# First MoE with two products a stage instead of three, and w2 times w_out folded into one matrix on the chip

## The chip, the cores and the metric

The kernel runs on one core of a Trainium2 chip. The metric is the device time of one execution in microseconds. A core has TensorE (matrix products), the vector engine (DVE), ScalarE (ACT), GpSimd (POOL) and SyncE (SP), each with a queue of its own that it works off in order; they wait for each other by semaphores.

## The reference

Three layers follow each other. The first is a linear attention with a decaying complex state, over 4 batches, 8 heads, 768 steps and head size 48. Its output, 3072 tokens of 384 numbers, goes into the first MoE, which the change is about, and the result into the second MoE, where each token goes to one of 8 experts.

```python
def _moe_ref(x, w1, w2, w3, w_out):
    h = np.maximum(np.maximum(x @ w1, x @ w2), x @ w3)
    return (h @ w_out).astype(np.float32)
```

Here x is 3072 x 384, w1, w2 and w3 are 384 x 768, w_out is 768 x 384. The weights come in as 64-bit floats. All is computed in 32 bits.

## The kernel before, in words

The program has two phases. In `phase1` the 3072 tokens are worked off as 12 units of 256 tokens (`NU`, `W`): attention, then the first MoE. In `phase2` the second MoE runs in blocks of tokens of one expert. The change touches `phase1` alone.

A unit passes `front` (the scale of the decay), `mid` and `back` (running products of the decay, the vector engine's share, which end in the tile `QK`), DMAs that lay `QK` out by head as `S`, and `attn`, twice, for 128 tokens each. In `attn` TensorE turns keys (`pk`, copied to `kt`), forms scores (`pa`, masked by the vector engine into `at`), the state (`pT`) and the output (`py`). The output leaves as two parts: `xhi`, rounded to the format fp32r, and the rest `xlo`. Products in fp32r are used in threes (high x high, high x low, low x high), so that three of them do for one in full fp32.

`moe1` computes a unit's first MoE in three stages `f2` of 256 hidden units. For each of the three weights `m` and each half `f` of the stage, `mm` issues 9 products (3 pairs of parts x 3 blocks of 128 inputs) of 128 x 128 weights by 256 tokens into a PSUM tile `ph`. ScalarE copies the first `ph` to `h`, the vector engine takes two maxima. In stages 0 and 1 (`SPLIT` is 2) `h` is rounded to `hhi`, the vector engine subtracts it (`hlo`), and 3 products per block with w_out's parts `wohi`, `wolo` add to `px`; in stage 2 the product with `wo` is in plain fp32. `px` has 392 columns: 384 outputs and 8 (`pG`) that give the second MoE's logits. ScalarE takes it out to `x1s`, and a DMA writes it to memory, from where the second MoE gathers its tokens.

```python
for n, (w, x, i) in enumerate((w, x, i) for w, x in ((self.whi, xhi), (self.wlo, xhi), (self.whi, xlo))
                              for i in range(3)):
    t.matmul(o, w[m, i][:, c], x[:, i], start=n == 0, stop=n == 8)
```

`weights` runs at the start. It loads 24 blocks of 128 x 384 64-bit numbers (6 of w_out, 18 of the three weights), puts each together as 32-bit floats on ScalarE and the vector engine (`sg`, `f`, `h`: sign, exponent, fraction), and splits 22 of them: ScalarE rounds (`hi`), TensorE forms the block minus `hi` in PSUM (`pd`), ScalarE takes that out (`rest`). It also turns w_out (`pwt`, `wt`) for the 8 extra columns.

Nothing is issued in the order of the code. A `Recorder` keeps all calls of `phase1`, a planner sorts them per engine by a list of keys, and `BIAS` shifts the keys of kinds of operations (a name of a tile and an engine's letter). Where the plan has TensorE idle for long, `keep_warm` (line 627) puts in products of the identity. Every instruction that the planner issues has line 368 in the profile.

Of the kernel before, what the change touches and what calls it, by code (L numbers as in the profile page):

```python
# [9 lines left out]
F32 = mybir.dt.float32  # L10
F32R = mybir.dt.float32r
# [3 lines left out]
AF = mybir.ActivationFunctionType  # L15
# [6 lines left out]
W = 256  # L22
# [3 lines left out]
DM = H * D  # L26
# [5 lines left out]
L = 8  # L32
# [91 lines left out]
class Recorder:  # L124
# [203 lines left out]
    def issue(self):  # L328
# [30 lines left out]
        for i in seq:  # L359
# [9 lines left out]
        return max(end)  # L369

    ENGINES = "vector", "scalar", "tensor", "gpsimd", "sync"
    BIAS = {"Gs": 1.84, "QKrg": -1.81, "Sg": 1.17, "Ss": 0.07, "Tss": 0.78, "Xv": 0.43, "arenv": 0.65, "cvhv": 0.53,
            "embss": -0.15, "fms": 2.46, "fmv": 3.34, "fyv": 0.76, "h_s": 0.7, "h_v": -0.65, "kt_s": -0.33, "pa_t": 1.07,
            "ph__t": -0.59, "pk_t": 1.3, "px__t": 0.15, "rrs": -0.38, "rrv": -0.75, "rwhig": -0.62, "rwlog": 1.88,
            "sav": -0.63, "slott": 2.08, "whi_s": 0.47, "wlo_s": 1.99, "xhis": 1.21, "xss": 0.26}
    PASSES, WAIT, LANES = 4, 130.0, 8
    START = {"vector": 1600.0, "gpsimd": 2200.0, "scalar": 2500.0, "sync": 1000.0}
    WINDOW = 4096 / 1.2
# [4 lines left out]
class Prog:  # L383
# [325 lines left out]
    def weights(self, split=True):  # L709
# [17 lines left out]
        spots = [(m, i) for i in range(3) for m in range(3)]  # L727
        todo = [(self.io["wo"][i], None, i, None) for i in range(6)]
        todo += [(self.io["w123"][m, i, :, c:c + n], m, i, c) for m, i in spots for c in (0, n)]
        sq = self.tl(pm, [128, 2 * W], "h", 2, "embsq")[:E, :DM]  # L730
        nrm, sr = [self.tl(pm, [E, 1], nm, 1, nm) for nm in ("nrm", "nrms")]
        s.activation(sq, emb, AF.Square, accum_out=nrm)
# [9 lines left out]
        ring, first = 0, 2 * self.SPLIT if split else 0  # L742
        for k, (src, m, i, c) in enumerate(todo):

            spot = None
            if split and m is not None:
# [24 lines left out]
            whole = m is None and i >= first  # L771
            o = self.wo[:, i - first, :DM] if whole else f if split else self.w[:, m, i, c:c + n]
            v.scalar_tensor_tensor(o.bitcast(I32), raw[:, :, 0], 29, h, op0=ALU.logical_shift_right, op1=ALU.bitwise_or)
            if split and not whole:
                if m is not None and c == 0:
# [3 lines left out]
                hi, rest = (self.wohi[:, i, :DM], self.wolo[:, i, :DM]) if m is None else \  # L779
                    (self.whi[m, i][:, c:c + n], self.wlo[m, i][:, c:c + n])  # L780
                s.copy(hi, f)
                pd = self.tl(self.pf, [128, n], "h", 3, f"pd{k}")
                with q.group():
                    t.matmul(pd, self.ident, f, start=True, stop=False)
                    t.matmul(pd, self.minus, hi, start=False, stop=True)
                s.copy(rest, pd)
            if m is None:

                if i == 0:
                    pG = self.tl(self.pf, [128, 6, E], "x1", 2, "pG")  # L790
                pt = self.tl(self.pf, [128, 3, 128], "h", 3, f"pwt{k}")
                for j in range(3):
                    t.transpose(pt[:, j], o[:, j * 128:(j + 1) * 128], self.ident)
                wt = self.tl(pm, [128, 3, 128], "h", 2, f"wt{k}")
                s.copy(wt, pt)
                for j in range(3):
                    t.matmul(pG[:, i], wt[:, j], enT[:, j], start=j == 0, stop=j == 2)
            if m is None and i == 5:
                if first:
                    s.copy(self.wohi[:, :, DM:], pG[:, :first])  # L800
                    v.tensor_sub(self.wolo[:, :, DM:], pG[:, :first], self.wohi[:, :, DM:].bitcast(F32))
                if first < 6:
                    v.tensor_copy(self.wo[:, :, DM:], pG[:, first:])

    def sqrt_small(self, new, out, x, n):

# [11 lines left out]
    def moe1(self, u):  # L818
# [5 lines left out]
        def mm(o, m, f):  # L824
            c = slice(f * 128, (f + 1) * 128)
            with q.group():
                for n, (w, x, i) in enumerate((w, x, i) for w, x in ((self.whi, xhi), (self.wlo, xhi), (self.whi, xlo))
                                              for i in range(3)):
                    t.matmul(o, w[m, i][:, c], x[:, i], start=n == 0, stop=n == 8)
        px = [self.tl(self.pf, [128, XC], "x1", 2, f"px1_{u}_{i}") for i in range(2)]  # L830
        for f2 in range(3):
            ps = []
            for m in range(3):
                ps.append(self.tl(self.pf, [128, 2, W], "h", 3, f"ph{u}_{f2}_{m}"))
                for f in range(2):
                    mm(ps[m][:, f], m, 2 * f2 + f)
            h = self.tl(pm, [128, 2, W], "h", 2, f"h{u}_{f2}")
            key, q.key = q.key, u + self.KEYS["max"]
            s.copy(h, ps[0])
            v.tensor_max(h, ps[1], h)  # L840
            v.tensor_max(h, ps[2], h)
            if f2 >= self.SPLIT:
                q.key = key
                for tt in range(2):
                    with q.group():
                        for f in range(2):
                            t.matmul(px[tt], h[:, f, tt * 128:tt * 128 + 128], self.wo[:, 2 * (f2 - self.SPLIT) + f],
                                     start=f2 + f == 0, stop=f2 + f == 3)
                continue
            hi = self.tl(pm, [128, 2, W], "hhi", 1, f"hhi{u}_{f2}", F32R)  # L850
            s.copy(hi, h)
            lo = self.tl(pm, [128, 2, W], "h", 2, f"hlo{u}_{f2}", F32R)
            v.tensor_sub(lo, h, hi.bitcast(F32))
            q.key = key
            for tt in range(2):
                with q.group():
                    for f in range(2):
                        ts = slice(tt * 128, tt * 128 + 128)
                        wh, wl = self.wohi[:, 2 * f2 + f], self.wolo[:, 2 * f2 + f]
                        for k, (a, b) in enumerate(((hi, wh), (hi, wl), (lo, wh))):  # L860
                            t.matmul(px[tt], a[:, f, ts], b, start=f2 + f + k == 0, stop=f2 + f + k == 5)
# [188 lines left out]
    def phase1(self):  # L1050
        nc, tc = self.nc, self.tc
        with ExitStack() as ctx:
# [9 lines left out]
            self.wo = mw.tile([128, 6 - 2 * self.SPLIT, XC], F32, name="wo")  # L1062
            self.wohi = mw.tile([128, 2 * self.SPLIT, XC], F32R, name="wohi")
            self.wolo = mw.tile([128, 2 * self.SPLIT, XC], F32R, name="wolo")
# [660 lines left out]
def host_layout(i):  # L1725
    f = np.ascontiguousarray

    def tr(x):
# [10 lines left out]
    perm = [h * D + e for h, e in XROWS]  # L1739

    w123 = np.stack([i[f"moe_w{n}"][perm].reshape(3, 128, FF) for n in (1, 2, 3)]).view(np.int64)
    wo = i["moe_w_out"].reshape(6, 128, DM).view(np.int64)
    return {
        "a": f(a), "qk": f(qk), "v": f(v), "w123": f(w123), "wo": f(wo),
        "emb": f(i["moe2_expert_emb"]),
        "tau": f(i["moe2_tau"]).reshape(1, 1),
        "w21": f(i["moe2_w1"].reshape(E, DM // 128, 128, FF2).transpose(0, 2, 1, 3)).reshape(E, 128, -1),
# [14 lines left out]
```

## Time and profile before

| | us |
|---|---|
| median of 3 runs | 809.39 (806.94 to 810.66) |
| the profiled execution | 811.25 |
| its span, first to last instruction | 809.4 |
| busy: TensorE / vector engine / ScalarE / GpSimd | 750.9 / 630.2 / 445.2 / 100.5 |
| mean granted TensorE clock | 0.977 |

The span is what the trace covers; 1.85 us of the execution lie outside. "Busy" is the time in which at least one instruction of the engine ran. The trace's products overlap each other (one of 392 columns lasts 0.34 us, and the next starts sooner): what one costs is the distance from one start to the next. PEld is TensorE's loading of weights, PEclk its granted clock (1.00 is 2.4 GHz).

### The profile page before, as it was taken

The page shows a single profiled execution, that of the slowest core. Times are in us where ns is not written, and L with a number is a line of the kernel's source. Part 1 is how long each engine was busy: PE and PEld are TensorE (multiplying, and loading weights), DVE is VectorE, ACT ScalarE, POOL GpSimd, SP SyncE. Part 2 cuts the span into 40 slices and gives each one's busy share as a digit, 9 for nine tenths or more (in the row PEclk, how much of TensorE's full clock was granted, in tenths as well). Part 3 has the DMA queues.
Part 4 walks back from the last instruction along what each step waited for, and adds up shares of the span by engine and source line. Part 5 has one row for each costly group of instructions (what it writes and reads, how often), then busy time and mean ns, then how long its engine had stood idle before and what let it go on. Part 6 is the DMA issues. An engine that isn't in the chain of part 4 may idle for free. (4 is left out here: it accounts for less than half of the span.)

```text
span 809.4 us, 19242 instructions
## 1 busy us (share of the span) xinstructions
PE 750.9 (93%) x7705; PEld 690.7 (85%) x7705; DVE 630.2 (78%) x1244; ACT 445.2 (55%) x1018; POOL 100.5 (12%) x156
## 2 busy tenths in 40 slices
PE   1757899999999999999999999999999999999996
PEld 0635789989898989999898989889989898989885
DVE  8999999999999999999988822659996455555420
ACT  8998746646647465665355341228545456554521
POOL 6301000000000000000000000021113312223111
PEclk9778999999999999999999999999999999999998
DMA  9706262571717345261624060051029694782500
GB/s 360 286 1 157 38 157 65 137 184 32 186 52 150 93 108 135 66 143 59 151 70 102 14 110 2 21 216 41 28 81 420 217 387 145 255 341 74 179 21 25
DMA packets 28754, 107.46 MB, mean 133 GB/s; under 512 B 5060, under 2 KB 8179, under 8 KB 25568
## 3 DMA queue, kind: packets, MB, share of 16 engines
q1 hardware_dynamic: 20432, 77.55, 32.2%
q0 software_dynamic: 7952, 28.21, 10.6%
q8 instruction: 62, 1.02, 0.5%
q10 hardware_dynamic: 272, 0.39, 0.2%
q14 instruction: 36, 0.29, 0.1%
HBM read 96.35 MB, written 10.62 MB: 132 GB/s over the span
## 5 line engine op out<-in xcount | busy, mean ns | idle before, releaser
L368 PE MATMUL ph<-xhi,whi 128*128 128x256 f32 x648 | 118.4, 291 | 0.4 <-DVE h L368 0.4
L368 PE MATMUL ph<-xlo,whi 128*128 128x256 f32 x648 | 113.0, 283 | 0.6 <-DVE xlo L368 0.6
L368 PE MATMUL ph<-xhi,wlo 128*128 128x256 f32 x648 | 112.7, 283 | 0.0
L368 PEld LDWEIGHTS ph<-xhi,whi 128*128 128x128 f32 x648 | 93.3, 191 | 6.9 <-issue 3.5
L368 PEld LDWEIGHTS ph<-xlo,whi 128*128 128x128 f32 x648 | 93.1, 192 | 1.0 <-DVE xlo L368 1.0
L368 PEld LDWEIGHTS ph<-xhi,wlo 128*128 128x128 f32 x648 | 93.0, 191 | 0.0
L1312 PE MATMUL ph<-xh,w1s 128*128 128x256 f32 x264 | 77.7, 294 | 0.0
L1274 DVE TENSOR_TENSOR w2l<-queue_q_buf,w2h 128x768 fp32r<-128x768 f32 x52 | 47.9, 955 | 37.3 <-ACT w2h L1273 37.3
L1312 PE MATMUL ph<-xh,w1l 128*128 128x256 f32 x264 | 75.4, 286 | 0.0
L1312 PE MATMUL ph<-xl,w1s 128*128 128x256 f32 x264 | 75.3, 285 | 0.0
L1328 PE MATMUL py<-w2h,hlo 128*128 128x384 f32 x200 | 67.1, 336 | 3.0 <-DVE hlo L1317 3.0
L1328 PE MATMUL py<-w2h,hhi 128*128 128x384 f32 x200 | 68.5, 343 | 0.0
L1328 PE MATMUL py<-w2l,hhi 128*128 128x384 f32 x200 | 67.1, 335 | 0.0
L368 DVE TENSOR_TENSOR h<-ph,h 128x512 f32<-128x512 f32 x72 | 49.5, 688 | 16.4 <-PE ph L368 15.0
L368 POOL DMA_DIRECT2D v<-v x24 | 13.0, 540 | 391.5 <-PE py L368 389.6
L1317 DVE SCALAR_TENSOR_TENSOR hlo<-ph,hhi 128x512 fp32r<-128x512 f32 x50 | 34.3, 687 | 32.7 <-ACT hhi L1316 32.6
L1316 ACT ACTIVATE hhi<-ph 128x512 fp32r<-128x512 f32 x50 | 29.9, 598 | 48.5 <-PE ph L1312 48.3
L1312 PEld LDWEIGHTS ph<-xh,w1s 128*128 128x128 f32 x264 | 51.2, 194 | 3.8 <-issue 3.1
L1312 PEld LDWEIGHTS ph<-xh,w1l 128*128 128x128 f32 x264 | 51.2, 194 | 0.5
L1312 PEld LDWEIGHTS ph<-xl,w1s 128*128 128x128 f32 x264 | 51.2, 194 | 0.0
L368 PE MATMUL pa<-S 112*128 112x128 f32 x384 | 49.1, 277 | 1.3 <-DVE at L368 0.7
L1273 ACT CAST w2h<-queue_q_buf 128x768 fp32r x52 | 40.7, 832 | 16.6 <-PE py L1328 15.5
(401 smaller groups left out, 1818.2 us busy)
## 6 DMA issues: line engine op xcount, KB each, us to landing
queue_q_buf<-w SPq DMA_DIRECT2D x26, 1536.0 KB
S<-QK SPq DMA_DIRECT2D x46, 289.1 KB
X<-a SPq DMA_DIRECT2D x11, 768.0 KB
QKr<-qk SPq DMA_DIRECT2D x11, 768.0 KB
w1m<-w SPq DMA_DIRECT2D x5, 1536.0 KB
w2m<-w SPq DMA_DIRECT2D x5, 1536.0 KB
v<-v POOLq DMA_DIRECT2D x24, 224.0 KB, 4.4
x1d<-x1s SPq DMA_DIRECT2D x22, 192.0 KB
```

Source lines behind the costliest of these rows:

```text
L368: getattr(getattr(self.nc, c[0]), c[1])(*c[2], **c[3])
L1273: s.copy(hi, b[:, c])
L1274: v.tensor_sub(lo, bv[:, c], hi.bitcast(F32))
L1312: t.matmul(ph[:, f], a, b, start=o == 0, stop=o == len(ops) - 1)
L1316: s.activation(hi, ph, AF.Relu).ins,
L1317: v.scalar_tensor_tensor(lo, ph, 0.0, hi.bitcast(F32), op0=ALU.max, op1=ALU.subtract).ins]
L1328: t.matmul(py, a[:, f, r], c[:, k % 4], start=o == 0, stop=o == 3 * KF - 1)
```

## The change

For each element max(a, b, c) = b + max(0, a - b, c - b). So h w_out = x (w2 w_out) + max(0, x (w1 - w2), x (w3 - w2)) w_out. The kernel now forms V = w2 w_out (384 x 392, with the 8 extra columns) on the chip, as parts `vhi` and `vlo`, and keeps w1 - w2 and w3 - w2 in place of the weights. The host hands in w2 turned (`w2t`), still as 64-bit floats. In `weights` the six blocks of w2 are converted first, the twelve of w1 and w3 then, and the six of w_out last. A difference is formed in PSUM: the identity times the block, plus three turned products of w2's blocks by -1. `rest` rounds it from PSUM (`hi`), adds -hi with one product, and takes the rest out. w_out is kept whole, and four of its six blocks also in two parts, formed by ScalarE and the vector engine. V takes 18 products in plain fp32.

In `moe1` there are two `ph` a stage. ScalarE's copy of the first becomes a relu; the vector engine takes one maximum. `by_v` adds x V to `px`, 18 products a unit: first in the unit, for unit 0 last (`late`). `BIAS` is another table, so the order is made anew.

```diff
@@ weights @@
-        todo = [(self.io["wo"][i], None, i, None) for i in range(6)]
+        out = [(self.io["wo"][i], None, i, None) for i in range(6)]
+        if split:
+            spots = [(m, i) for i in range(3) for m in (0, 2)]
+            todo = [(self.io["w2t"][f], 1, f, None) for f in range(6)]
...
+        todo = todo + out
...
+        def rest(hi, lo, ps):
+            s.copy(hi, ps)
+            t.matmul(ps, self.minus, hi, start=False, stop=True, skip_group_check=True)
+            s.copy(lo, ps)
...
-                s.copy(hi, f)
                 pd = self.tl(self.pf, [128, n], "h", 3, f"pd{k}")
                 with q.group():
-                    t.matmul(pd, self.ident, f, start=True, stop=False)
-                    t.matmul(pd, self.minus, hi, start=False, stop=True)
-                s.copy(rest, pd)
+                    t.matmul(pd, self.ident, f, start=True, stop=True)
+                    for b in range(3):
+                        t.matmul(pd[:, b * 128:(b + 1) * 128], w2t[:, c // 128 + b, i * 128:(i + 1) * 128],
+                                 self.minus.bitcast(F32), start=False, stop=True, skip_group_check=True)
+                rest(self.whi[m, i][:, c:c + n], self.wlo[m, i][:, c:c + n], pd)
...
+        for f in range(2 * self.SPLIT):
+            s.copy(self.wohi[:, f], self.wo[:, f])
+            v.tensor_sub(self.wolo[:, f], self.wo[:, f], self.wohi[:, f].bitcast(F32))
+        for i in range(3):
+            pw = self.tl(self.pf, [128, XC], "h", 3, f"pw{i}")
+            with q.group():
+                for f in range(6):
+                    t.matmul(pw, w2t[:, f, i * 128:(i + 1) * 128], self.wo[:, f], start=f == 0, stop=f == 5)
+            rest(self.vhi[:, i], self.vlo[:, i], pw)
@@ moe1 @@
+        late = u == 0
+        def by_v():
+            for tt in range(2):
+                ts = slice(tt * 128, tt * 128 + 128)
+                with q.group():
+                    for n, (x, w, i) in enumerate((x, w, i) for x, w in ((xhi, self.vhi), (xhi, self.vlo), (xlo, self.vhi))
+                                                  for i in range(3)):
+                        t.matmul(px[tt], x[:, i, ts], w[:, i], start=n == 0 and not late, stop=n == 8 and late)
+        if not late:
+            by_v()
         for f2 in range(3):
             ps = []
-            for m in range(3):
+            for m in (0, 2):
...
-            s.copy(h, ps[0])
+            s.activation(h, ps[0], AF.Relu)
             v.tensor_max(h, ps[1], h)
-            v.tensor_max(h, ps[2], h)
...
+        if late:
+            by_v()
```

**What moves.** First TensorE, at the start of unit 0's attention. `pd` are splits of weights, `pwt` and `pG` belong to w_out's 8 extra columns, `pw` are V's products, `pk` and `pa` unit 0's turned keys and scores. Before:

```order
L368 MATMUL pk_1_265<-ident,S_142 128x112 x4
L368 MATMUL pa_1_269<-S_142 128x128 x4
L368 MATMUL pd_221<-cvh_154,ident 128x384
L368 MATMUL pd_221<-whi_219,minus 128x384
L368 MATMUL pk_0_263<-ident,S_142 128x112 x4
L368 MATMUL pd_223<-cvh_155,ident 128x384
L368 MATMUL pd_223<-whi_219,minus 128x384
L368 MATMUL pa_0_267<-S_142 128x128 x4
```

Of the change:

```order
L368 MATMUL pwt_214<-ident,wo 128x128 x3
L368 MATMUL pG<-enT,wt_213 128x8 x2
L368 MATMUL pG<-enT,wt_215 128x8 x3
L368 MATMUL pw_216<-wo,w2t 128x392 x6
L368 MATMUL pw_217<-wo,w2t 128x392 x6
L368 MATMUL pk_0_247<-ident,S_144 128x112 x4
L368 MATMUL pw_218<-wo,w2t 128x392 x6
L368 MATMUL pa_0_251<-S_144 128x128 x4
L368 MATMUL pk_1_249<-ident,S_144 128x112 x4
```

Unit 0's attention ran between the splits of the last weights; now all splits, w_out and two thirds of V stand ahead of it.

Then the vector engine, from the last `QK` of unit 11 on. `hlo`, `h` are unit 9's and unit 10's first MoE, `at` masked scores, `xlo` the low part of unit 10's input. Before:

```order
L368 TENSOR_TENSOR QK_1029<-rr_1028,X_891 128x6x128 x2
L368 TENSOR_TENSOR hlo_1_931<-h_1_929,hhi_1_930 128x512
L368 TENSOR_TENSOR at_0_982<-pa_0_981,mask 128x512
L368 TENSOR_TENSOR at_1_984<-pa_1_983,mask 128x512
L368 TENSOR_TENSOR h_2_935<-ph_2_1_933,h_2_935 128x512
L368 TENSOR_TENSOR h_2_935<-ph_2_2_934,h_2_935 128x512
L368 SCALAR_TENSOR_TENSOR xlo_975<-py_985,xhi_974 128x3x128
L368 TENSOR_TENSOR h_0_994<-ph_0_1_992,h_0_994 128x512
L368 TENSOR_TENSOR h_0_994<-ph_0_2_993,h_0_994 128x512
```

Of the change:

```order
L368 TENSOR_TENSOR QK_980<-rr_979,X_848 128x6x128 x2
L368 TENSOR_TENSOR hlo_1_886<-h_1_884,hhi_1_885 128x512
L368 TENSOR_TENSOR at_0_936<-pa_0_935,mask 128x512
L368 TENSOR_TENSOR at_1_938<-pa_1_937,mask 128x512
L368 TENSOR_TENSOR h_2_889<-ph_2_2_888,h_2_889 128x512
L368 SCALAR_TENSOR_TENSOR xlo_929<-py_939,xhi_928 128x3x128
L368 TENSOR_TENSOR at_0_989<-pa_0_988,mask 128x512
L368 TENSOR_TENSOR at_1_991<-pa_1_990,mask 128x512
L368 TENSOR_TENSOR h_0_947<-ph_0_2_946,h_0_947 128x512
```

The same work stands at the same place behind unit 11's `QK`, with one maximum a stage instead of two; unit 11's first scores have moved ahead of unit 10's maxima. In the whole queue 58 maxima stood ahead of this `QK`, and 29 do now.

## Rows read from the trace of the kernel before

**Rows 1.** By stage: us, busy PE PEld DVE ACT POOL, PEclk, DMA share, GB/s.
```profile
0.00:98.50 98.50, 60.45 (x468) 46.38 (x469) 91.70 (x221) 86.59 (x218) 24.11 (x75) 0.86 0.48 170
98.50:545.40 446.90, 439.63 (x5369) 408.41 (x5369) 385.27 (x761) 225.52 (x603) 15.87 (x25) 1.00 0.42 102
545.40:809.40 264.00, 250.83 (x1872) 235.92 (x1870) 153.26 (x264) 133.13 (x200) 60.53 (x56) 0.98 0.45 170
```

**Rows 2.** Timeline of TensorE where stages meet: start, us, engine, line, instruction, [idle before].
```profile
98.26 0.44 PE L368 MATMUL pd<-whi,minus 128*128 128x384 f32 x1 [0.44 <-ACT whi L368]
98.54 0.52 PE L368 MATMUL ph<-xhi,whi 128*128 128x256 f32 x3
...
545.38 10.88 PE L1312 MATMUL ph<-xT,w1s 128*128 128x128 f32 x96
```

**Rows 3.** Timeline of TensorE in the first MoE of units 9 and 11.
```profile
442.65 0.52 PE L368 MATMUL ph<-xhi,whi 128*128 128x256 f32 x3
443.01 0.52 PE L368 MATMUL ph<-xhi,wlo 128*128 128x256 f32 x3
...
532.83 0.34 PE L368 MATMUL px<-wohi,hhi 128*128 128x392 f32 x1
...
534.80 0.34 PE L368 MATMUL px<-wohi,hlo 128*128 128x392 f32 x1
...
540.36 2.79 PE L368 MATMUL px<-wo,h 128*128 128x392 f32 x8
542.99 0.49 PE L368 MATMUL pxg<-ident,xg 128*128 128x128 f32 x3
```

**Rows 4.** Vector engine's groups to 540 us: busy us, mean ns | idle before.
```profile
L368 DVE TENSOR_TENSOR h<-ph,h 128x512 f32<-128x512 f32 x72 | 49.5, 688 | 16.4 <-PE ph L368 15.0 <-ACT h L368 0.7
...
L368 DVE TENSOR_TENSOR hlo<-h,hhi 128x512 fp32r<-128x512 f32 x24 | 16.5, 689 | 8.2 <-ACT hhi L368 8.2
```

**Rows 5.** Timeline of the vector engine, a maximum and the instruction behind it.
```profile
414.65 0.68 DVE L368 TENSOR_TENSOR h<-ph,h 128x512 f32<-128x512 f32 x1
415.25 0.95 DVE L368 TENSOR_TENSOR QKr<-QKr,rr 128x768 f32<-128x768 f32 x1
```

**Rows 6.** Timeline of the vector engine, `QK` of units 0 and 11.
```profile
64.03 0.96 DVE L368 TENSOR_TENSOR QK<-rr,X 128x768 f32<-128x768 f32 x1
...
462.19 1.83 DVE L368 TENSOR_TENSOR QK<-rr,X 128x768 f32<-128x768 f32 x2
...
474.37 0.56 DVE L368 SCALAR_TENSOR_TENSOR xlo<-py,xhi 128x384 fp32r<-128x384 f32 x1 [4.50 <-ACT xhi L368]
```

**Rows 7.** Timeline of TensorE in the first stage.
```profile
24.80 0.78 PE L368 MATMUL pwt<-ident,S 128*128 128x128 f32 x3
25.41 0.29 PE L368 MATMUL pG<-enT,wt 128*128 128x8 f32 x2
...
71.16 0.81 PE L368 MATMUL pd<-S,ident 128*128 128x384 f32 x2
71.51 0.63 PE L368 MATMUL pd<-whi,minus 128*128 128x384 f32 x1
```

**Rows 8.** TensorE by 5 us in the first stage: busy, clock, DMA.
```profile
35.00:40.00 5.00, 4.98 (x26) 0.50 0.01 3
70.00:75.00 5.00, 2.57 (x15) 1.00 1.03 216
```

**Rows 9.** Timeline of the vector engine at the end of routing.
```profile
532.28 0.17 DVE L368 TENSOR_SCALAR srcrow<-arena 128x8 int32<-128x8 f32 x1
...
542.25 3.41 DVE L1266 COPY w1s<-queue_q_buf 128x1536 f32 x2 [2.80 <-DMA xg<-x1d,srcrow]
```

**Rows 10.** Groups of ScalarE: copy, rounding, and the second MoE's relu.
```profile
L1316 ACT ACTIVATE hhi<-ph 128x512 fp32r<-128x512 f32 x50 | 29.9, 598 | 48.5 <-PE ph L1312 48.3
L368 ACT COPY h<-ph 128x512 f32<-128x512 f32 x36 | 21.1, 585 | 35.2 <-DVE hlo L368 21.4 <-PE ph L368 12.1 <-DVE G L368 1.6
L368 ACT CAST hhi<-h 128x512 fp32r<-128x512 f32 x24 | 14.9, 619 | 41.3 <-PE px L368 23.1 <-DVE h L368 17.9
```

More of the change, by code (lines that the diff above doesn't have):

```diff
@@ L371 @@
     ENGINES = "vector", "scalar", "tensor", "gpsimd", "sync"
[L372 to L375, printed above, removed]
+    BIAS = {"QKrg": 0.03, "QKrv": -1.09, "QKs": -0.04, "Sg": 0.06, "Ss": -0.01, "Sv": -0.98, "Xg": -1.06, "arenv": -0.17,
+            "embss": 0.11, "embv": -0.35, "enTv": 0.06, "end_s": -0.27, "fms": 0.76, "fmv": -0.06, "fys": -0.13,
+            "hlo_v": -0.76, "lgs": 0.57, "nrmss": -0.19, "nrmsv": -0.1, "rrv": -0.58, "rwlog": 0.04, "sqrev": -0.19,
+            "takev": -0.17, "whi_s": -0.52, "wlo_s": 0.39, "wohis": -0.43, "wov": -0.9, "wts": -0.37, "xhis": -0.42}
     PASSES, WAIT, LANES = 4, 130.0, 8
@@ L726, in weights @@
         hs = [part(4 + i) for i in range(3)] + [self.tl(pm, [128, XC], "x1s", 2, f"cvh{i}")[:, :n] for i in range(2)]
-        spots = [(m, i) for i in range(3) for m in range(3)]
-        todo = [(self.io["wo"][i], None, i, None) for i in range(6)]
+        out = [(self.io["wo"][i], None, i, None) for i in range(6)]
+        if split:
+            spots = [(m, i) for i in range(3) for m in (0, 2)]
+            todo = [(self.io["w2t"][f], 1, f, None) for f in range(6)]
+            w2t = self.tl(self.pp, [128, 3, L, 3 * NR], "X", 3, "w2t").rearrange("p c l b -> p (c l b)")
+            w2t = w2t.rearrange("p (f d) -> p f d", f=6)
+        else:
+            spots, todo = [(m, i) for m in range(3) for i in range(3)], []
         todo += [(self.io["w123"][m, i, :, c:c + n], m, i, c) for m, i in spots for c in (0, n)]
+        todo = todo + out
         sq = self.tl(pm, [128, 2 * W], "h", 2, "embsq")[:E, :DM]
@@ L741, in weights @@
         v.tensor_copy(enT, ps)
-        ring, first = 0, 2 * self.SPLIT if split else 0
+        ring = 0
+        def rest(hi, lo, ps):
+            s.copy(hi, ps)
+            t.matmul(ps, self.minus, hi, start=False, stop=True, skip_group_check=True)
+            s.copy(lo, ps)
         for k, (src, m, i, c) in enumerate(todo):
             spot = None
-            if split and m is not None:
+            if split and c is not None:
                 j = spots.index((m, i)) + (c > 0)
@@ L770, in weights @@
             v.scalar_tensor_tensor(h, h, 3, sg, op0=ALU.logical_shift_left, op1=ALU.bitwise_or)
-            whole = m is None and i >= first
-            o = self.wo[:, i - first, :DM] if whole else f if split else self.w[:, m, i, c:c + n]
+            o = self.wo[:, i, :DM] if m is None else f if split and c is not None else w2t[:, i] if split else \
+                self.w[:, m, i, c:c + n]
             v.scalar_tensor_tensor(o.bitcast(I32), raw[:, :, 0], 29, h, op0=ALU.logical_shift_right, op1=ALU.bitwise_or)
-            if split and not whole:
-                if m is not None and c == 0:
+            if split and c is not None:
+                if c == 0:
                     j = spots.index((m, i))
@@ L778, in weights @@
                                                       for x in ("hi", "lo")]
-                hi, rest = (self.wohi[:, i, :DM], self.wolo[:, i, :DM]) if m is None else \
-                    (self.whi[m, i][:, c:c + n], self.wlo[m, i][:, c:c + n])
-                s.copy(hi, f)
                 pd = self.tl(self.pf, [128, n], "h", 3, f"pd{k}")
                 with q.group():
-                    t.matmul(pd, self.ident, f, start=True, stop=False)
-                    t.matmul(pd, self.minus, hi, start=False, stop=True)
-                s.copy(rest, pd)
+                    t.matmul(pd, self.ident, f, start=True, stop=True)
[3 more added lines that the diff above has]
+                rest(self.whi[m, i][:, c:c + n], self.wlo[m, i][:, c:c + n], pd)
             if m is None:
@@ L798, in weights @@
             if m is None and i == 5:
[L799 to L803, printed above, removed]
+                v.tensor_copy(self.wo[:, :, DM:], pG)
+        if not split:
+            return
+        for f in range(2 * self.SPLIT):
[7 more added lines that the diff above has]
+            rest(self.vhi[:, i], self.vlo[:, i], pw)
     def sqrt_small(self, new, out, x, n):
@@ L830, in moe1 @@
         px = [self.tl(self.pf, [128, XC], "x1", 2, f"px1_{u}_{i}") for i in range(2)]
+        late = u == 0
[8 more added lines that the diff above has]
+            by_v()
         for f2 in range(3):
             ps = []
-            for m in range(3):
+            for m in (0, 2):
                 ps.append(self.tl(self.pf, [128, 2, W], "h", 3, f"ph{u}_{f2}_{m}"))
                 for f in range(2):
-                    mm(ps[m][:, f], m, 2 * f2 + f)
+                    mm(ps[-1][:, f], m, 2 * f2 + f)
             h = self.tl(pm, [128, 2, W], "h", 2, f"h{u}_{f2}")
             key, q.key = q.key, u + self.KEYS["max"]
-            s.copy(h, ps[0])
+            s.activation(h, ps[0], AF.Relu)
             v.tensor_max(h, ps[1], h)
-            v.tensor_max(h, ps[2], h)
[L842 to L853, printed above, removed]
+            if f2 < self.SPLIT:
+                hi = self.tl(pm, [128, 2, W], "hhi", 1, f"hhi{u}_{f2}", F32R)
+                s.copy(hi, h)
+                lo = self.tl(pm, [128, 2, W], "h", 2, f"hlo{u}_{f2}", F32R)
+                v.tensor_sub(lo, h, hi.bitcast(F32))
             q.key = key
@@ L858, in moe1 @@
                         ts = slice(tt * 128, tt * 128 + 128)
-                        wh, wl = self.wohi[:, 2 * f2 + f], self.wolo[:, 2 * f2 + f]
-                        for k, (a, b) in enumerate(((hi, wh), (hi, wl), (lo, wh))):
-                            t.matmul(px[tt], a[:, f, ts], b, start=f2 + f + k == 0, stop=f2 + f + k == 5)
+                        if f2 < self.SPLIT:
+                            wh, wl = self.wohi[:, 2 * f2 + f], self.wolo[:, 2 * f2 + f]
+                            terms = (hi, wh), (hi, wl), (lo, wh)
+                        else:
+                            terms = (h, self.wo[:, 2 * f2 + f]),
+                        for k, (a, b) in enumerate(terms):
+                            t.matmul(px[tt], a[:, f, ts], b, start=late and f2 + f + k == 0,
+                                     stop=not late and f2 + f == 3 and k == len(terms) - 1)
+        if late:
+            by_v()
         for tt in range(2):
@@ L1061, in phase1 @@
             self.mw, self.whi, self.wlo = mw, {}, {}
-            self.wo = mw.tile([128, 6 - 2 * self.SPLIT, XC], F32, name="wo")
-            self.wohi = mw.tile([128, 2 * self.SPLIT, XC], F32R, name="wohi")
-            self.wolo = mw.tile([128, 2 * self.SPLIT, XC], F32R, name="wolo")
+            self.wo = mw.tile([128, 6, XC], F32, name="wo")
+            self.vhi, self.vlo = [mw.tile([128, 3, XC], F32R, name=n) for n in ("vhi", "vlo")]
+            if self.SPLIT:
+                self.wohi, self.wolo = [mw.tile([128, 2 * self.SPLIT, XC], F32R, name=n) for n in ("wohi", "wolo")]
             self.minus = self.tl(self.pm, [128, 128], "hhi", 1, "minus", F32R)
@@ L1741, in host_layout @@
     w123 = np.stack([i[f"moe_w{n}"][perm].reshape(3, 128, FF) for n in (1, 2, 3)]).view(np.int64)
+    w2t = f(i["moe_w2"][perm].T).reshape(6, 128, DM).view(np.int64)
     wo = i["moe_w_out"].reshape(6, 128, DM).view(np.int64)
     return {
-        "a": f(a), "qk": f(qk), "v": f(v), "w123": f(w123), "wo": f(wo),
+        "a": f(a), "qk": f(qk), "v": f(v), "w123": f(w123), "w2t": w2t, "wo": f(wo),
         "emb": f(i["moe2_expert_emb"]),
```

## The prediction, made before the change had run

> **What bounds the kernel now.** I read the busy time by stage first [rows 1], then the timeline of TensorE for where the stages meet and how fast it issues [rows 2, 3], then the groups and the timeline of the vector engine [rows 4 to 6], then the start of the program [rows 7, 8], and last the hand-over to the second MoE [rows 9].
>
> There are three stages. Up to 98.5 us the weights are converted and unit 0's attention runs: the vector engine is busy 91.7 of 98.5 us and ScalarE 86.6, TensorE only 60 [rows 1]. From 98.5, where the first `ph` product of unit 0 starts right behind the last split of a weight, to 545.4, where the first product of the second MoE starts [rows 2], TensorE is busy 439.6 of 446.9 us [rows 1]. So this stage, attention and first MoE of the units, goes at TensorE's pace; a product that is taken out of it shortens it, as long as its operands keep coming. They come from the vector engine, and that is the second thing to see: 385.3 us busy in the same stage, but nearly full until its last scan work (`QK` of unit 11) ends at 464 [rows 6], and idle for most of the 81 us after. It has next to no room either. The third stage, 264 us, is the second MoE; the change leaves its code and order alone, and I take it as it is.
>
> **TensorE, part by part.** One `ph` product takes 0.12 us: three start 0.36 us apart as a row of three [rows 3]. A unit has 3 stages of 3 weights, 2 halves and 9 products, 162 in all; without w2 it has 108. Removed: 54 x 0.12 = 6.48 us a unit. Added: x V, for 2 halves of the tokens 9 products of 392 columns each. Products of that form start 0.179 us apart (11 steps from 532.83 to 534.80 [rows 3]), so 18 x 0.179 = 3.22 us. Net -3.26 us a unit, **-39.1 us for 12 units**, all on the engine that sets the stage. The order as built bears it out: each unit has 12 groups of `ph`, not 18, and the 18 products by V.
>
> **The vector engine.** One of two maxima a stage goes: 36 in all. A maximum lasts 688 ns [rows 4], but the next instruction starts 0.60 us after it [rows 5], so 36 x 0.60 = 21.6 us. Four subtractions of 392 columns come in for w_out's low part; a subtraction of 512 lasts 689 ns [rows 4], so they cost at most 2.8. The loads, bit operations and their count (24 blocks of 384 columns) stay. What counts is what stands ahead of unit 11's `QK` in the queue: 58 maxima before, 29 now, so 17.4 us less, and 2.4 more by four subtractions at 0.60: **-15 us**. `QK` of unit 11 then ends at about 449 instead of 464, and up to 4 us sooner if the vector engine's own waits in that stretch (on products and on ScalarE) shrink with a TensorE that is less behind.
>
> **ScalarE.** Copy becomes relu on the same tile: 585 ns for the copy, 598 for a relu of 128x512 out of PSUM in the second MoE [rows 10]; 36 x 13 ns on an engine that is busy 225.5 of 446.9 us [rows 1] costs nothing. In the start, 22 blocks were split by two copies each; now 12 are, plus 4 copies for w_out and 6 for V: ten fewer. If this cover were gone it would be 10 x 0.5 us, a gain.
>
> **The start.** Here something is added in front. Each weight difference needs three turned products by -1 (36 of them); three turns start 0.61 us before the next instruction [rows 7], so 36 x 0.2 = 7.3 us. Ten pairs of split products go, each about 0.8 to 1.0 us (0.35 to the second, which lasts 0.63 [rows 7]): 8 to 10 us. These cancel. New is V: 18 products of w2's blocks with w_out in plain fp32. Such a product is two records of about 0.33 us (8 records for 4 products in the 2.63 us from 540.36 to 542.99 [rows 3]), so 18 x 0.66 = **11.8 us**. Twelve of the 18 stand ahead of unit 0's first turns (`pk`), and unit 0's products by V are put at the end of its first MoE. The conversion of w_out is now the last and its last block stands six bit operations behind `QK` of unit 0, which ended at 65 [rows 6]; so V cannot start before about 70 us. Not hidden at the least 0 (TensorE is busy only 60 of 98.5 us in this stage), at the most 11.8 at the full clock. The vector engine has some thirty instructions of unit 1 in its queue for that time, but then stands at the mask of unit 0's scores. I take **+6**, the middle, since the work ahead is on both sides.
>
> **The end of the stage.** Unit 11's first MoE is 3.26 us shorter, and the routing of the first 22 tiles runs beside it: its rows are ready at 532.3 and the weights of the second MoE at 542.25 [rows 9], so that only some 3 us lie between the weights and the first product at 545.4. Routing does not get shorter with unit 11's products. It starts a little sooner (the order sets part of unit 11's attention behind unit 10's last products), so 0 to 3 us of the gain are lost here; I take 2.
>
> **The sum.** By TensorE alone: -39.1 + 6 + 2 = -31. By the vector engine: the low half of unit 10's input (`xlo`) stands behind unit 11's `QK` in its queue, and came at 474.4, 71 us ahead of the second MoE [rows 6, 2]. In the change its `QK` ends at 445 to 449, `xlo` follows five instructions later, at about 453; from there two first MoEs are left, 71 - 6.5 = 64.5 us. That puts the second MoE at 517.5, a gain of 28. Both bounds are so near each other that the later rules: **-28 us**. The profiled execution took 811.25 us, of which 1.85 lie around its span of 809.4; it stands 1.9 above the median of 809.39. So 783 for it, and **781 us** against the median.
>
> **The rivals.**
> - *TensorE alone sets the pace.* V is wholly hidden in the start and the vector engine sheds its waits: -39.1 + 2 = -37, so 772 (768 to 776). For it: TensorE's idle time in the first stage. Against it: the vector engine has 15 to 19 us less to do ahead of unit 11, not 37.
> - *The vector engine alone sets it*, and its waits stay: -15 and nothing more, 794 (790 to 800). For it: it is full until 464. Against it: some of its idle time there was waiting for products.
> - *V runs at half the clock.* From 35 to 40 us TensorE was busy 4.98 of 5 us and had a granted clock of 0.50, the 1.2 GHz level, while 70 to 75 us shows 1.00, the 2.4 GHz level, with it busy 2.57 of 5 [rows 8]. If V falls into such a stretch it takes 23.6 us, 12 more, and unit 0's attention comes as much later: 793 (787 to 797). The Trainium skill (TensorE: Matmul & The Clock Gate, Part 1) has it the other way: the clock is throttled by default and sustained activity releases it. By that rule V, the densest work of the start, would be at the full level and this rival falls. The row from 35 to 40 us speaks against it: there a busy engine stayed at the lower level for all five us.
> - *Slower: the chain behind the maximum is laid bare.* With two products a stage instead of three, TensorE has 36 `ph` products of the next stage (4.3 us), not 54 (6.5 us), to run while the maximum (0.69), the rounding (0.62) and the subtraction (0.69) go by, 2.0 us [rows 4, 10]. If queues on ScalarE and the vector engine stretch that by as much as the cover lost, each of the 24 split stages waits up to 2.0 us: +48, 829. It decides from 28 / 24 = 1.2 us a stage. Against it: 4.3 us of cover for 2.0 us of work, V's products and the attention of the next unit are there as well, and a third PSUM buffer is now free for running ahead.
> - *No change to be measured* would need the half clock and a part of the bared chain together.
>
> **How the numbers follow.** Forecast (776 to 787) 0.55; TensorE alone 0.18; half clock 0.13; vector engine alone 0.08; slower 0.03; within 0.5% 0.03. Half a per cent, 4 us, is about what a measurement of this kernel can tell from no change. So faster 0.94, same 0.03, slower 0.03. The range 768 to 795 takes in the forecast, the first rival and most of the next two, and leaves out about 0.15.
>
> **What would show each step.** In the profile after: `ph` with 432 of each of three kinds instead of 648; products by V, 216 in all, 0.18 us apart; TensorE still busy nine tenths or more from the first `ph` to the second MoE. First `ph` product at 100 to 108 us instead of 98.5: if it is at 115 or later, the start was mis-sized, and the granted clock while V runs tells whether by the clock. Unit 11's `QK` at 445 to 449: if at 455, the vector engine was mis-sized. Second MoE at 515 to 520 instead of 545.4, and 262 to 266 us from there to the end: if the third stage is longer, the cause is outside this argument. Waits of `ph` and `px` for the maximum or the low half, each over 1 us in most stages, would show the slower rival. The prediction is wrong if TensorE has more than 20 us of idle time between the first `ph` and the second MoE.

## The result, and the profile after

| us | before | after |
|---|---|---|
| median | 810.02 (4 runs, 806.94 to 811.65) | 782.96 (4 runs, 782.07 to 787.72) |
| the profiled execution, its span | 811.25, 809.4 | 783.0, 781.2 |
| first `ph` of unit 0 | 98.54 | 107.79 |
| last `QK` of unit 11 (start) | 462.19 | 440.79 |
| first product of the second MoE | 545.38 | 517.91 |

The ratio of after to before is 0.9682, 95% interval 0.9633 to 0.9731: faster by 27 us. 781 was forecast.

The windows by stage of the kernel after, as in [rows 1]; the last two cut the second stage at unit 11's `QK`:

```profile
0.00:107.80 107.80, 71.68 (x534) 55.36 (x534) 96.52 (x217) 81.66 (x199) 24.23 (x75) 0.89 0.48 159
...
107.80:517.90 410.10, 402.17 (x4938) 370.18 (x4937) 357.63 (x732) 226.31 (x609) 16.30 (x25) 1.00 0.44 110
517.90:781.20 263.30, 249.37 (x1872) 234.45 (x1870) 153.44 (x264) 133.19 (x200) 61.13 (x56) 0.99 0.45 171
...
107.80:440.80 333.00, 327.97 (x4142) 302.42 (x4141) 324.08 (x643) 203.34 (x542) 10.19 (x19) 0.99 0.47 115
440.80:517.90 77.10, 74.21 (x798) 67.77 (x798) 33.55 (x90) 22.97 (x68) 6.11 (x6) 1.00 0.31 92
```

The same view of the kernel before, up to its last `QK`:

```profile
98.50:462.20 363.70, 358.99 (x4509) 334.19 (x4509) 347.01 (x665) 202.52 (x535) 10.22 (x19) 1.00 0.44 106
```

The second stage became 36.8 us shorter (446.9 to 410.1), the first 9.3 longer, the third is as it was (264.0, 263.3): -28.2 in the span. TensorE is still busy 98% of the second stage, and the vector engine 324 of 333 us up to its last `QK`. So both look full; ScalarE, at 203 of 333, does not.

TensorE after: the stages' meeting points, and the products by V.

```profile
107.79 0.60 PE L368 MATMUL ph<-xhi,whi 128*128 128x256 f32 x3
108.23 0.52 PE L368 MATMUL ph<-xhi,wlo 128*128 128x256 f32 x3
112.41 0.87 PE L368 MATMUL ph<-xlo,whi 128*128 128x256 f32 x3 [3.66 <-DVE xlo L368]
113.08 0.84 PE L368 MATMUL ph<-xhi,whi 128*128 128x256 f32 x3
113.72 0.84 PE L368 MATMUL ph<-xhi,wlo 128*128 128x256 f32 x3
...
467.38 0.70 PE L368 MATMUL px<-vlo,xhi 128*128 128x392 f32 x3
467.91 0.70 PE L368 MATMUL px<-vhi,xlo 128*128 128x392 f32 x3
468.45 0.52 PE L368 MATMUL ph<-xhi,whi 128*128 128x256 f32 x3
...
517.91 1.28 PE L1342 MATMUL ph<-xT,w1s 128*128 128x128 f32 x10
```

Three products by V start 0.54 us apart, 0.18 each, as forecast, and there are 216 of them, and 432 of each kind of `ph`. Compared with [rows 2], the start has become worse: the first `ph` comes 9.3 us later, and its third group then waits 3.66 us for `xlo`.

The vector engine after, at unit 11's `QK` and unit 10's `xlo`:

```profile
440.79 1.83 DVE L368 TENSOR_TENSOR QK<-rr,X 128x768 f32<-128x768 f32 x2
...
452.34 0.56 DVE L368 SCALAR_TENSOR_TENSOR xlo<-py,xhi 128x384 fp32r<-128x384 f32 x1 [3.74 <-ACT xhi L368]
```

`QK` is 21.4 us sooner than in [rows 6], more than the 15 forecast, and `xlo` is 22.0 us sooner. At 452.3 `xlo` is where it was forecast (453), but not by the forecast's way: it starts 9.7 us after the end of `QK` (442.6), where the prediction had 4. It waits 3.74 us for `xhi`, whose `py` comes from TensorE; before, the distance was 10.35 us (464.02 to 474.37) and the wait 4.50 [rows 6]. TensorE's longest waits between the first `ph` and the second MoE (engine, what waited, for what: us in total, times, longest):

```profile
PE ph L368 <- DVE xlo L368: 3.7, 1, 3.7
PE pxg L1319 <- ACT xT L368: 1.5, 1, 1.5
PE slots L368 <- DVE pos L368: 0.8, 1, 0.8
```

Four more, of 0.6 us at most, follow; none is for a maximum or a low half `hlo`. So the first reading: the time came from the second stage, and TensorE and the vector engine both gave it. Theory one is the prediction's: the two stand level, and the later rules. Its rivals: TensorE alone rules, or the vector engine alone, with room on the other.

### The profile page after: what moved, and what is told of

It is laid out like the page before. It is cut to its first block, busy times and chain, and to the rows that moved or that the text cites. A ratio compares the mean times of both kernels' runs of the same rounds, so it can differ in the third digit from the quotient of the medians.

```text
span 781.2 us, 18475 instructions
## 1 busy us (share of the span) xinstructions
PE 723.2 (93%) x7338; PEld 660.0 (84%) x7338; DVE 607.6 (78%) x1211; ACT 441.2 (56%) x1007; POOL 101.7 (13%) x156
## 5 line engine op out<-in xcount | busy, mean ns | idle before, releaser
L368 PE MATMUL ph<-xhi,whi 128*128 128x256 f32 x432 | 82.4, 300 | 0.0
L368 PE MATMUL ph<-xlo,whi 128*128 128x256 f32 x432 | 75.8, 285 | 3.7 <-DVE xlo L368 3.7
L368 PE MATMUL ph<-xhi,wlo 128*128 128x256 f32 x432 | 75.4, 283 | 0.0
L368 PEld LDWEIGHTS ph<-xhi,whi 128*128 128x128 f32 x432 | 63.5, 191 | 8.5 <-issue 6.0
L368 PEld LDWEIGHTS ph<-xlo,whi 128*128 128x128 f32 x432 | 62.5, 193 | 3.9 <-DVE xlo L368 3.9
L368 PEld LDWEIGHTS ph<-xhi,wlo 128*128 128x128 f32 x432 | 62.2, 191 | 0.0
L368 PE MATMUL pa<-S 112*128 112x128 f32 x384 | 51.0, 276 | 2.2 <-DVE at L368 1.4
L368 PEld LDWEIGHTS pa<-S 112*128 112x128 f32 x384 | 47.2, 190 | 4.4 <-DVE at L368 2.4
```

The source lines that it names most:

```text
L368: getattr(getattr(self.nc, c[0]), c[1])(*c[2], **c[3])
```

## The experiments

All start from the changed kernel. In those that repeat or leave out an operation the edit is in the loop that issues the finished plan, so that the order of everything else stands. Medians of four to six runs are compared (both_less ran once); differences under 2 us are not told apart here. The other columns come from one trace each. The first `ph` alone differs from 106.1 to 108.0 us between traces whose start is the same, instruction by instruction (the change, max_twice, ph_twice, max_none, v_high_only, both_less, relu_twice).

| us | time | first `ph` | last `QK` | second MoE |
|---|---|---|---|---|
| the change | 782.96 | 107.8 | 440.8 | 517.9 |
| max_twice | 798.59 | 108.0 | 459.6 | 536.3 |
| ph_twice | 818.13 | 106.1 | 467.2 | 551.1 |
| max_none | | 106.5 | 438.0 | 515.5 |
| v_high_only | 779.11 | 107.0 | 439.6 | 513.5 |
| both_less | | 107.4 | 430.7 | 504.3 |
| v_short | | 106.5 | 440.4 | 517.1 |
| pw_twice | 793.23 | 120.8 | 450.3 | 527.5 |
| relu_twice | 783.93 | 106.5 | 440.6 | 518.1 |
| wide_warm | 781.18 | 106.7 | 439.1 | 516.2 |
| old_order | 782.0 | 111.0 | 439.5 | 516.6 |
| low2 | 793.8 | 114.4 | 448.3 | 526.7 |
| split1 | 789.05 | 104.0 | 440.6 | 523.5 |

Where no time stands, the routing after it was another one (v_short's third stage took 508 us), so only the time up to the second MoE is read.

**Work added to one engine.** The vector engine's maxima back, then TensorE's products:

```diff
-            for c in o.calls:
+            for c in o.calls * (2 if self.kind(o) == "h_v" else 1):
```

> Each of the 36 maxima is issued twice in place, the order of everything else kept: 36 x 0.60 = 21.6 us more for the vector engine, 17.4 of them (29) ahead of unit 11's QK. If the vector engine rules the stage (the later bound of the prediction): 797 to 805 against 783, unit 11's QK at 457 to 461 instead of 440.8. If TensorE rules and the vector engine has room: 783 to 787, QK later but the second MoE still at 516 to 522. A time between tells how much room there was.

Measured 798.59, ratio to the kernel before 0.984 (0.9794 to 0.9887). `QK` moved by 18.8 us and the second MoE by 18.4. Two maxima in a row, the instruction behind them, and the stretch up to unit 11's `QK`:

```profile
408.15 1.41 DVE L368 TENSOR_TENSOR h<-ph,h 128x512 f32<-128x512 f32 x2
409.48 0.55 DVE L368 TENSOR_TENSOR mc<-Ct,G 128x384 f32<-128x384 f32 x1
...
107.80:459.60 351.80, 333.19 (x4147) 303.71 (x4146) 343.39 (x671) 203.29 (x543) 10.19 (x19) 1.00 0.45 109
```

The pair takes 1.33 us to the next start, a single maximum 0.60 [rows 5]; a repeated one costs 0.73, not the 0.60 of the expectation, and 29 of them 21. Of these 18.8 arrived: the vector engine has about 2 us of room. TensorE, which had 5 us of idle time in this stretch, now has 18.6. The time moved by 15.6 only, since the second MoE took 260.7 us in this trace against 263.3; why, these runs don't tell.

```diff
+        again = [id(o) for o in self.ops if self.kind(o) == "ph__t" and len(o.calls) == 9][::4]
-            for c in o.calls:
+            for c in o.calls * (2 if id(o) in again else 1):
```

> In every stage of the first MoE the 9 products of the first weight and first half are issued twice: 27 x 0.12 = 3.24 us a unit, 38.9 us in all for TensorE, which is what the change took from it; the vector engine keeps its 36 maxima less. If TensorE stands level with the vector engine: 817 to 823 (38.9 less at most 5 us of room). If the vector engine rules and TensorE has room (10 us or more): below 812.

Measured 818.13, ratio 1.0075 (1.0052 to 1.0098): 35.2 us came back. The first `ph` and the second MoE:

```profile
106.07 0.60 PE L369 MATMUL ph<-xhi,whi 128*128 128x256 f32 x3
...
551.06 9.20 PE L1343 MATMUL ph<-xT,w1s 128*128 128x128 f32 x80 [1.18 <-ACT xT L369]
```

Between them lie 445.0 us against 410.1, 34.9 more, of 38.9 put in. TensorE has about 4 us of room. And it shows the parts of the change apart: with the vector engine's saving alone (and V at the start) the kernel is 0.75% slower than before, with TensorE's alone (max_twice) it wins 1.6%; only both give 3.2%.

**Work taken from one engine.**

```diff
-            for c in o.calls:
+            for c in o.calls * (self.kind(o) != "h_v"):
```

> The 36 maxima are left out (h is the relu of the first product alone, the second is computed and not used), the rest in its order. The vector engine loses 36 x 0.60 = 21.6 us, 17.4 ahead of unit 11's QK; putting 29 in moved that QK by +18.8 (max_twice). If the vector engine alone ruled and TensorE had room: 765 to 768, QK at 422 to 424. If TensorE is close behind: it has 5 us of idle time of 333 ahead of that QK, so 776 to 781, and its idle time there goes below 3 us.

```diff
+                if c[1] == "matmul" and len(o.calls) == 9 and self.kind(o) == "px__t" and not (c[3]["start"] or c[3]["stop"]):
+                    n = [x is c for x in o.calls].index(True)
+                    if n > 2:
+                        continue
```

> In each unit's products by V only high x high is kept, 3 of 9 a half (of unit 0's second group 4); the two terms with a low part are left out, so the output is less exact. 12 x 0.179 = 2.15 us a unit less for TensorE, 25.7 us in all; order as it was, nothing changes for the other engines. If TensorE rules: 757 to 761. If the vector engine rules: 779 to 783. Between, if both are near each other: the gain is what the vector engine leaves, its queue of unit 11's QK then ends ahead of where it did by as little as it had waited for products.

Each gave little: 21.6 us off the vector engine moved the second MoE by -2.4, 25.7 us off TensorE by -4.4 (779.11, ratio 0.9602, 0.9555 to 0.9649); 1.3 and 0.8 of that lie ahead of the first `ph`, where neither changes anything. The windows up to unit 11's `QK`, of max_none first:

```profile
106.50:438.00 331.50, 326.78 (x4140) 302.12 (x4139) 310.21 (x614) 202.91 (x541) 10.20 (x19) 0.99 0.48 115
```

and of v_high_only:

```profile
107.00:439.60 332.60, 311.08 (x4024) 281.49 (x4023) 323.75 (x643) 202.88 (x542) 10.20 (x19) 0.99 0.47 115
```

The stretch is as long in both, 332 us, and as in the change, 333. In the first the vector engine has 21 us of idle time and TensorE 5, in the second it is TensorE that has 21 and the vector engine 9; in the change these were 9 and 5. What TensorE waits for then, in v_high_only:

```profile
PE pa L372 <- DVE at L372: 7.8, 5, 2.0
...
PE ph L372 <- DVE xlo L372: 5.1, 3, 3.7
...
PE pa L372 <- ACT kt L372: 3.2, 4, 1.2
```

It waits above all for the vector engine's masks (7.8 us, in the change 0.5) and for `kt` from ScalarE (in the change no such wait is listed); of the 5.1 for low parts 3.66 are unit 0's, which the change has too. A TensorE that was 98% busy was not the only wall: taking work from it laid bare the other.

**Both.** The two edits together.

> max_none and v_high_only in one: the 36 maxima left out and the two low terms of the products by V too, order kept (the output is wrong, and the second MoE then routes other tokens, so only the time up to its first product is read, 517.9 us before this). Alone, the first moved unit 11's QK by -2.8 us and the second by -1.2. If the two engines stand level, each just behind the other, both out must give what neither gave alone: QK at 418 to 426 instead of 440.8 and the second MoE at 490 to 498. If a third thing holds the stage (ScalarE, a DMA): QK at 433 or later.

```profile
107.40:430.70 323.30, 310.55 (x4024) 281.52 (x4023) 309.09 (x614) 202.81 (x542) 10.19 (x19) 0.99 0.49 118
```

`QK` came at 430.7 and the second MoE at 504.3: -10.1 and -13.6, two to two and a half times the sum of the two alone (-4.0 and -6.8), which bears out that each stood behind the other, but less than the 15 to 28 expected: `QK` lies between the two expectations (418 to 426, 433 or later). Both engines now have 13 to 14 us of idle time in 323, so neither is full. Two of TensorE's waits in this stretch:

```profile
PE ph L371 <- DVE xlo L371: 4.9, 3, 3.6
PE pk L371 <- DMA S<-QK: 2.3, 3, 1.5
```

7.7 us of its waits are for the vector engine, 2.3 for the DMA that lays out `QK` (0.6 in the change). So a third thing, the DMA, has a small part here. Whether the rest comes from an order that was planned for longer work, these runs don't tell.

**The start.** V with 12 of its 18 products left out, and V twice:

```diff
+                if self.kind(o) == "pwt" and len(o.calls) == 6 and not (c[3]["start"] or c[3]["stop"]):
+                    continue
```

> Of the 18 products that form V at the start only 6 are kept (the first and last block of w_out; the output is then wrong by what is left out). Twelve go: 12 x 0.66 = 7.9 us at the full clock, 10.7 as they ran. If V lies on the path, as the +6 of the prediction has it: 772 to 777. If unit 0's attention comes sooner but the vector engine rules the queue up to unit 11's QK: first ph at 97 to 101 instead of 107.8, and still 780 to 783.

```diff
-            for c in o.calls:
+            for c in o.calls * (2 if self.kind(o) == "pwt" and len(o.calls) == 6 else 1):
```

> The 18 products of V are issued twice at the start, 12 to 15 us more for TensorE ahead of unit 0's scores. v_short, with 12 of them fewer, moved the second MoE by -0.8 us only. If V lies hidden with room to spare: 783 to 786. If it had just used up its cover (ScalarE's and the vector engine's own queues, which held unit 0's attention in v_short): 790 to 797, first ph at 117 to 121, with the vector engine idle at unit 0's masks.

TensorE in the change, where V's first two thirds end, and in v_short up to the rounding of V's last third:

```profile
76.70 10.72 PE L368 MATMUL pw<-wo,w2t 128*128 128x392 f32 x24 [0.30 <-DVE wo L368]
87.25 0.55 PE L368 MATMUL pk<-ident,S 112*128 112x112 f32 x4
...
82.29 0.59 PE L370 MATMUL pk<-ident,S 112*128 112x112 f32 x4
...
89.74 0.69 PE L370 MATMUL pw<-vhi,minus 128*128 128x392 f32 x1 [3.39 <-ACT vhi L370]
91.73 2.08 PE L370 MATMUL pa<-S 112*128 112x128 f32 x8 [1.30 <-ACT kt L370]
```

Unit 0's `pk` came 5 us sooner, and then TensorE waited for ScalarE: 3.39 us for `vhi`, the rounding of V's last third, and 1.30 for `kt`. ScalarE's queue in turn waits for the vector engine's work on unit 1. First `ph` -1.3, second MoE -0.8: both lie within what the start differs by itself, so no cost of these twelve products can be told apart. What V's other six products and its roundings cost was not tried. The vector engine in pw_twice:

```profile
88.99 0.96 DVE L368 TENSOR_TENSOR m<-X,C 128x768 f32<-128x768 f32 x1 [4.71 <-ACT C L368]
...
103.78 0.69 DVE L368 TENSOR_TENSOR at<-pa,mask 128x512 f32<-128x512 f32 x1 [5.72 <-PE pa L368]
```

A second V is not hidden: the vector engine stands at the mask, the first `ph` comes 13.0 us later, unit 11's `QK` 9.5, and the time moves to 793.23 (ratio 0.9775, 0.9747 to 0.9802). So V's products lie hidden, and have about used up their cover.

**The clock in the start.**

```diff
+                    self.wide = pG[:, 128:256]
...
         o = a[0][:, :min(128, a[0].shape[1])]
+        if o.shape[1] == E:
+            o = self.wide
```

> The keep-warm products that stand ahead of pG and pen, 8 columns wide, are made 128 wide, into unused columns of pG's bank. Nothing else moves. Theory A (the clock fell at 61 us and stayed at 0.50 to 81 because the products put in there were too narrow to count): the granted clock stays at 1.00, or near it, from 60 to 82 us, V's twelve products take 7.9 instead of 10.7 us, turns and pG ahead of them some 3 us less, first ph at 101 to 104 instead of 107.8, time 777 to 780. Theory B (the clock falls in the start anyway, or what is won there waits elsewhere): clock still 0.50 in that stretch or the time 782 to 786, with the wider products only adding up to 2 us.

TensorE by 5 us, from 60, after the change (columns as in [rows 8]):

```profile
60.00:65.00 5.00, 3.12 (x16) 2.94 (x16) 5.00 (x7) 5.00 (x12) 0.00 (x0) 0.64 0.25 79
65.00:70.00 5.00, 4.46 (x22) 4.37 (x22) 5.00 (x12) 1.32 (x4) 2.75 (x5) 0.50 0.86 267
70.00:75.00 5.00, 5.00 (x25) 4.80 (x24) 3.99 (x11) 1.54 (x4) 0.49 (x1) 0.50 1.02 260
75.00:80.00 5.00, 4.70 (x11) 3.15 (x12) 3.12 (x15) 3.58 (x10) 0.00 (x0) 0.50 0.84 153
80.00:85.00 5.00, 5.00 (x14) 2.77 (x13) 3.57 (x10) 1.54 (x4) 0.00 (x0) 0.81 0.05 10
```

and in wide_warm:

```profile
60.00:65.00 5.00, 2.30 (x17) 1.87 (x17) 5.00 (x8) 5.00 (x14) 0.00 (x0) 0.87 0.33 81
65.00:70.00 5.00, 5.00 (x24) 4.93 (x24) 5.00 (x13) 0.71 (x2) 3.06 (x6) 0.50 0.97 327
70.00:75.00 5.00, 5.00 (x25) 4.87 (x24) 2.85 (x8) 2.14 (x5) 0.17 (x1) 0.50 1.07 236
75.00:80.00 5.00, 4.70 (x9) 2.71 (x10) 4.10 (x19) 2.57 (x8) 0.00 (x0) 0.50 0.69 94
...
75.62 10.72 PE L368 MATMUL pw<-wo,w2t 128*128 128x392 f32 x24 [0.30 <-DVE wo L368]
```

Theory A fell: the clock went down somewhat later (0.87 against 0.64 from 60 to 65 us), but it stayed at 0.50 from 65 to 80 us, and V's first twelve products took 10.72 us in both. 781.18 (ratio 0.9642, 0.9591 to 0.9694) can't be told from the change.

**The order.** The old `BIAS` table on the new code:

```diff
-    BIAS = {"QKrg": 0.03, "QKrv": -1.09, "QKs": -0.04, "Sg": 0.06, "Ss": -0.01, "Sv": -0.98, "Xg": -1.06, "arenv": -0.17,
...
+    BIAS = {"Gs": 1.84, "QKrg": -1.81, "Sg": 1.17, "Ss": 0.07, "Tss": 0.78, "Xv": 0.43, "arenv": 0.65, "cvhv": 0.53,
...
```

> The new code with the old BIAS table, so that the order is planned by the old preferences. If the gain comes from the work that is taken out of TensorE and the vector engine: 781 to 790. If the new table carries a part of its own: above 795, with idle time of TensorE of more than 10 us beyond the 7.9 that it has between the first ph and the second MoE.

Measured 782.0 (ratio 0.9636, 0.959 to 0.9683). The gain is the work's, not the table's. Its first `ph` came at 111.0, without the wait for `xlo`, and its second MoE at 516.6.

**The slower rival.**

```diff
+            for c in o.calls * (2 if self.kind(o) == "h_s" else 1):
```

> ScalarE issues each relu of the first MoE twice, 36 x 0.5 us: the chain behind the maximum is 0.5 us longer in each stage. If two products a stage still cover that chain: 782 to 786. If it lies bare (the prediction's slower rival): 0.5 us for each of 24 to 36 stages, 795 to 801.

Measured 783.93 (ratio 0.9665, 0.9635 to 0.9694): the chain behind the maximum is covered, with about 0.5 us a stage to spare. In the trace ScalarE issues 72 relus instead of 36, 0.6 us each, so some 21 us more on it moved the time by 1.0 us: ScalarE is not a wall either.

**Two tries at a faster kernel**, both planned anew.

```diff
-    LOW = 1
+    LOW = 2
```

> The low part of a unit's second half of tokens is formed as that of the first is: one product by the identity on TensorE, taken out by ScalarE, instead of a subtraction on the vector engine; order planned anew. 12 x 0.47 us less for the vector engine (11 ahead of unit 11's QK, 5.2 us), 12 x 0.2 = 2.4 more for TensorE, 12 x 0.4 for ScalarE. If the vector engine rules: 776 to 780. If TensorE does: 783 to 787.

Measured 793.8 (ratio 0.9806, 0.9771 to 0.9842), outside both expectations. The plan put V into the middle of unit 0's attention and the first `ph` came at 114.4; from there to the second MoE it took 412.3 us against 410.1. So the loss is mostly the start's (6.6 us); what the edit itself is worth stays open.

```diff
-    SPLIT = 2
+    SPLIT = 1
```

> SPLIT 1 instead of 2: the second stage's product with w_out goes in plain fp32 too. Per unit 4 products of 0.66 us in place of 12 of 0.179, +0.48 us, 5.8 in all for TensorE; 12 roundings less for ScalarE and 12 subtractions (0.60) and two of w_out's four less for the vector engine, 7.2 + 1.2 us, about 7 of them ahead of unit 11's QK. If the vector engine rules: 775 to 779. If TensorE does: 785 to 790. Even between the two: 780 to 784.

Measured 789.05 (ratio 0.9754, 0.9716 to 0.9791): +6.1, close to the 5.8 that TensorE got more, but put together otherwise. The first `ph` came at 104.0, 3.8 us sooner, and from there to the second MoE it took 419.5 us, 9.4 more. The order is another one here too, so what the edit is worth stays open. Apart from v_high_only, which leaves out terms of the product, no kernel here beats the change by more than can be told apart.

## Why the prediction was right, step by step

- **TensorE, -39.1: right.** From the first `ph` to the second MoE its busy time went down by 37.5 us (439.6 to 402.2), though `ph` lost about 1.3 us there at half the clock (rows of three 0.64 apart from 113.08 on, not 0.36; granted clock 0.50 from 113 to 116 us). Its idle time there went from 7.3 to 7.9, 3.66 of it the wait for `xlo`. With the start's 9.3 the account closes: -37.5 + 0.7 + 9.3 = -27.5, where the prediction's sum by TensorE had -31.
- **The vector engine, -15: too small; it was -21.4.** Up to the last `QK` it was busy 438.7 us before and 420.6 after: -18.1, and its idle time went from 23.5 to 20.2, which the prediction had allowed for (up to 4). The maxima were priced rightly: where nothing is waited for, the next instruction starts about 0.60 us behind one, before and after. What the other 3.1 us of busy time are I can't place. `QK` ended at 442.6, ahead of 445 to 449.
- **From `QK` to the end: two slips that cancel, and luck.** The prediction let `xlo` follow 4 us after the end of `QK` (449 to 453), as if the queue were all that held it. [rows 6] has 10.35 us there, 4.50 of them a wait for `xhi`; the change has 9.7, with 3.74 of that wait. With the distance of [rows 6] its -15 would have put `xlo` at 459 and the second MoE at about 524, a gain of 22 us and not 28. `QK` came 6 us sooner than forecast and the distance was 6 us longer, so that `xlo` (452.3) and the second MoE (forecast at 517.5, measured 517.9) met their numbers. From `xlo` on it took 65.6 us, forecast 64.5.
- **"The two stand level": right, and shown.** ph_twice and max_twice leave TensorE about 4 us of room and the vector engine about 2, max_none and v_high_only say the same from the other side, and both_less shows that each stood behind the other. But the vector engine does not hold the stage through the place of `xlo` behind `QK`, as the sum had it: with more work on it (max_twice) TensorE waits all along the units, 18.6 us in place of 5 up to the last `QK`.
- **The start, +6: it was +9.3, and the cause is open.** Of V, twelve products cost nothing that can be told apart (v_short), while a second V moves the first `ph` by 13 us (pw_twice). The first `ph` was at 107.8, inside 100 to 108, but TensorE's steady work began at 112.4. In the trace `xlo` of unit 0 is issued at 111.80, with the vector engine busy from the end of `xhi` (106.17) on, on work of later units that stands ahead in its queue. That its place in the queue is the cause was not tried. With V in them and other orders, split1 and old_order have the first `ph` at 104.0 and 111.0 without a long wait behind it, so the order has a part in the start.
- **Routing, +2: not there.** From the weights to the first product 3.1 us lie before (542.25, 545.38 [rows 9, 2]) and after (514.83, 517.91):

```profile
514.83 3.41 DVE L1296 COPY w1s<-queue_q_buf 128x1536 f32 x2 [3.11 <-DMA xg<-x1d,srcrow]
```

- **Half the clock.** V's first twelve products did begin at it: 0.89 us each on the average instead of 0.66, some 2.8 us and not the rival's 12, in a place where they were hidden. As in [rows 8], from 65 to 80 us TensorE was busy 4.46, 5.00 and 4.70 of 5 us at the 1.2 GHz level, and the clock rose only while V ran, between 80 and 85 us. The rule of the Trainium skill (TensorE: Matmul & The Clock Gate, Part 1), that sustained activity releases the clock, is borne out here only in part: the clock did rise under V, but after 15 us of nearly full work at the lower level.
- **TensorE alone, the vector engine alone:** the first fell with max_twice, the second with ph_twice. **The bared chain** fell with relu_twice.

## What to carry to other kernels

An engine that is 98% busy need not be the only wall: here 25.7 us less for it gave 4. Before a change that takes work from the fullest engine, look how much the next one has to do ahead of the same point, and count what the change takes from each; the smaller saving bounds the forecast. Repeating an operation in place, with the order kept, measures an engine's room within a run, once the price of the repeat is read from its own trace (0.73 us here, not 0.60); leaving work out measures only the distance to the next wall. And check each step of a forecast against a row even where its end comes true: here two slips of 6 us cancelled.

## What was not expected of the hardware

TensorE had the 1.2 GHz level from 65 to 80 us while it was busy 14.2 of these 15 us, after an idle gap of 1.88 us that ended at 61.98, and it did so in wide_warm too. And a second issue of the same maximum on the vector engine, into the tile that it has just written, cost 0.73 us (1.33 for the pair) where 0.60 lies between the start of a single one and the next start.
